# Nine matmuls on zeros ahead of the first real one, in place of fourteen

## The chip, the cores and the metric

The kernel runs on one core of one Trainium2 chip. The metric is the time of one execution on the device, in microseconds (us). The engines are TensorE (PE: matmuls; PEld: the loads of its stationary operand), VectorE (DVE), ScalarE (ACT), GpSimd (POOL) and the queue that issues most transfers (SP).

## The reference, cut to what matters

Attention through 32 landmarks (means over groups of 18 tokens), for 8 batches of 8 heads with 576 tokens of 64 channels, then a mixture of 8 experts in which each of the 4608 tokens goes to one expert:

```python
def _attn_ref(q, k, v):                       # each (8, 8, 576, 64)
    q_lm = q.reshape(B, H, m, S // m, D).mean(axis=3)
    k_lm = k.reshape(B, H, m, S // m, D).mean(axis=3)
    A = sm(q, k_lm)
    Bm = sm(q_lm, k_lm)
    C = sm(q_lm, k)
    Z = Bm.transpose(0, 1, 3, 2) / (norm1(Bm) * norminf(Bm) + 1e-06)
    for _ in range(6):
        Z = 2 * Z - Z @ Bm @ Z
    return A @ Z @ C @ v

def _moe_ref(x, w_gate, w1, w2):              # x (4608, 512); w1 (8, 512, 1024); w2 (8, 1024, 512)
    logits = x @ w_gate
    expert_idx = np.argmax(logits, axis=1)
    for e in range(E):
        mask = expert_idx == e
        h = np.maximum(x[mask] @ w1[e], 0.0)
        out[mask] = gate_w[mask, None] * (h @ w2[e])
    return out
```

(Here `norm1` and `norminf` stand for the two matrix norms, and `sm` for a softmax over scaled products.)

## The kernel before, in words

The kernel has two parts. In the first, attention, the work comes in quads: a quad is four heads of one batch, so there are 16 quads, and two quads make the pair of one batch. In the second, the experts, blocks of 128 tokens of one expert go through its two weight matrices.

Attention runs in periods. In period `i` the generator `front` turns keys and queries of quad `i` (line 123: three PE transposes of 96 columns for each head, by a product with the identity; line 124: ACT copies them out of PSUM, with two buffers of the tile `ps_tp`); `middle` makes the landmark means and the score products of quad `i-1` (lines 143, 171, 176) and their softmaxes; `values` multiplies quad `i-2` with its values (lines 255, 261, 269, 275); `back` iterates the inverse of a pair (line 319: eight products in turn, each followed by work of DVE and ACT on the tile `rp`) and applies it (line 359); `final` makes the rows of a pair (line 394: twelve matmuls; line 395: ACT copies them; line 400: SP stores them into `xs`). Keys, queries and values of a quad come in three transfers of 576 KB (line 112, tiles `ld_k`, `ld_q`, `ld_v`, two buffers each, so that the load for quad `i` waits until quad `i-2` has been read); the first two quads' come in halves of two heads. The values of the first quad are issued behind the queries of the third.

The order on each engine in this part isn't written out by hand. `merge` deals the steps of the generators of one period in proportion, each with a priority (a boost for `back` and `final`: `BOOST`), and the framework's scheduler (`schedule_with_timeline_sim=True`) then orders the instructions of every engine by its own estimate of when each can start. From the end of the periods on, the order of PE and SP, and later of the other engines, is the program's own (`manual_schedule`).

At the very beginning, while the first keys are on the way, PE multiplies a tile of zeros with itself. Nothing reads the products. They stand in the constructor of `Routing` (lines 480 to 484), and their number is a constant of the module, at line 35:

```python
        x = zero.bitcast(BF16)
        ps = self.p_ch.tile([128, 512], F32, name="ps_ch")
        for _ in range(WARM):
            nc.tensor.matmul(ps, lhsT=x[:, :128], rhs=x[:, :512], start=True, stop=True)
```

`ps` is a buffer of the pool `p_ch`, whose next user is the first product of line 319. `zero` is set by DVE (line 479) and is stored once (line 485) to clear a table.

Of the kernel before, what the change touches and what calls it, by code (L numbers as in the profile page):

```python
# [31 lines left out]
TAIL = 1  # L32
AHEAD = 0
WAIT = 0
WARM = 14
ROWS, FETCH = 15, 16


# [418 lines left out]
class Routing:  # L457


    def __init__(self, tc, ctx, front, psum, order):  # L460
# [21 lines left out]
# [3 lines that stand above are left out]
# [556 lines left out]
```

## Time and profile before

| | us |
|---|---|
| three runs | 695.89, 700.67, 702.92 (median 700.67) |
| the profiled execution | 696.69 |
| its span, first to last instruction | 694.9 |
| mean granted TensorE clock | 0.967 of 2.4 GHz |
| PE busy | 648.9 (93%) |
| DVE busy | 521.8 (75%) |
| ACT busy | 400.6 (58%) |
| POOL busy | 342.9 (49%) |

The execution is 1.8 us longer than its span: what lies ahead of the first and behind the last instruction. A busy share is that of instructions under way; the granted clock is a share of full speed, 2.4 GHz, and has two levels, 1.00 and 0.50 (1.2 GHz); a mean between them tells how much of a stretch lay at either.

### The profile page before, as it was taken

What the parts mean: (1) busy time and instruction counts of PE and PEld (TensorE: products, weight loads), DVE (VectorE), ACT (ScalarE), POOL (GpSimd) and SP (SyncE); (2) the same over time, 40 slices, a digit from 0 to 9 for tenths busy, and PEclk for the clock granted to TensorE, in tenths of its full rate; (3) what the DMA queues carried; (4) which work ended last, traced back from release to release, by engine and by line L of the source; (5) the groups of instructions that cost most, each with busy time, mean ns of one, the idle gap of its engine ahead of it and who ended that gap; (6) DMA issues with size and microseconds to landing.
All of it is one profiled execution on the core that took longest, in us unless ns stands there. A gap on an engine that the chain in (4) does not pass through costs nothing.

```text
span 694.9 us, 13825 instructions
## 1 busy us (share of the span) xinstructions
PE 648.9 (93%) x4489; PEld 510.0 (73%) x4489; DVE 521.8 (75%) x1409; ACT 400.6 (58%) x997; POOL 342.9 (49%) x371
## 2 busy tenths in 40 slices
PE   8899989999699868989999999999999999999996
PEld 4676757667476646867888888888888888888884
DVE  4788857769887977667699779857699699866653
ACT  4776656556655654345567576645467467544542
POOL 4554546357347263777546354453535445351231
PEclk9999989789889998999999999999999999999999
DMA  9996876668823550255143333411144243310010
GB/s 212 246 225 162 191 167 145 147 136 161 235 75 107 166 117 7 65 195 186 62 154 112 122 114 106 158 54 38 61 153 142 79 157 105 110 62 32 31 50 29
DMA packets 45482, 84.70 MB, mean 122 GB/s; under 512 B 8050, under 2 KB 26484, under 8 KB 45376
## 3 DMA queue, kind: packets, MB, share of 16 engines
q1 hardware_dynamic: 35328, 63.24, 34.4%
q0 software_dynamic: 10048, 20.29, 9.2%
q8 instruction: 38, 0.62, 0.4%
q14 instruction: 68, 0.56, 0.3%
HBM read 64.29 MB, written 19.73 MB: 121 GB/s over the span
## 4 chain that ended last, share of the span: by engine, by line
PE 46%; DMA 3%; issue 3%; POOL 1%; DVE 1%; ACT 0%; POOLq 0%; DVEq 0%
PE ps_fi L820 12%; PE ps_ch L820 12%; PE ps_fr L820 11%; PE ps_tp L820 11%; DMA xe<-xs,read 3%; DVE h L840 0%; POOL xg L788 0%; POOL out_dram L851 0%; POOL xe L788 0%; DVE buf L801 0%; DVE ht_lo L806 0%; ACT ht_hi L803 0%; POOLq L886 0%; POOLq L851 0%; DVEq L801 0%
## 5 line engine op out<-in xcount | busy, mean ns | idle before, releaser
L851 POOL DMA_INDIRECT out_dram<-buf,write x38 | 38.6, 1016 | 166.9 <-ACTq L777 141.0
L788 POOL DMA_INDIRECT xe<-xs,read x84 | 87.4, 1040 | 25.7 <-issue 23.8
L788 POOL DMA_INDIRECT xg<-xs,read x80 | 83.3, 1042 | 30.4 <-issue 23.0
L803 ACT CAST ht_hi<-buf 128x512 fp32r<-128x512 f32 x76 | 47.1, 622 | 71.5 <-DVE buf L801 70.5
L840 DVE TENSOR_SCALAR h<-ps_tp 32x256 f32<-32x256 f32 x152 | 64.2, 422 | 27.2 <-PE ps_tp L820 24.9
L840 DVE TENSOR_SCALAR h<-ps_fi 32x256 f32<-32x256 f32 x144 | 60.8, 422 | 28.5 <-PE ps_fi L820 26.1
L838 ACT ACTIVATE h<-ps_tp 32x256 f32<-32x256 f32 x152 | 57.1, 376 | 41.3 <-PE ps_tp L820 37.5
L838 ACT ACTIVATE h<-ps_fi 32x256 f32<-32x256 f32 x144 | 54.1, 376 | 34.5 <-PE ps_fi L820 30.7
L820 PE MATMUL ps_ch<-whi,ht_hi 128*128 128x512 f32 x152 | 59.8, 394 | 2.2 <-ACTq L777 2.2
L394 PE MATMUL ps_fi<-w,at 128*96 128x264 f32 x160 | 52.6, 424 | 9.4 <-DVE l L398 7.7
L820 PE MATMUL ps_fr<-whi,ht_hi 128*128 128x512 f32 x152 | 60.8, 400 | 0.0
L820 PE MATMUL ps_fr<-wlo,ht_hi 128*128 128x512 f32 x152 | 60.1, 395 | 0.0
L820 PE MATMUL ps_fr<-whi,ht_lo 128*128 128x512 f32 x152 | 59.8, 394 | 0.0
L820 PE MATMUL ps_ch<-wlo,ht_hi 128*128 128x512 f32 x152 | 59.5, 391 | 0.0
L820 PE MATMUL ps_ch<-whi,ht_lo 128*128 128x512 f32 x152 | 59.2, 389 | 0.0
L564 POOL DMA_INDIRECT order<-i_tok,l_at x48 | 44.8, 934 | 28.8 <-issue 10.9
L801 DVE STREAM_TRANSPOSE buf<-h 128x512 f32<-128x512 f32 x76 | 49.7, 690 | 5.7 <-DMA out_dram<-buf,write 1.9
L806 DVE TENSOR_TENSOR ht_lo<-buf,ht_hi 128x512 fp32r<-128x512 f32 x76 | 51.0, 692 | 3.7 <-ACT ht_hi L803 0.2
L765 DVE TENSOR_TENSOR wlo<-raw,whi 128x512 fp32r<-128x512 f32 (+1 forms) x64 | 48.8, 819 | 3.2 <-ACT whi L764 3.2
L820 PE MATMUL ps_tp<-whi,xt_hi 128*128 128x512 f32 x152 | 48.7, 401 | 2.2 <-ACTq L777 2.2
L820 PE MATMUL ps_tp<-whi,xt_lo 128*128 128x512 f32 x152 | 47.9, 396 | 0.0
L820 PE MATMUL ps_tp<-wlo,xt_hi 128*128 128x512 f32 x152 | 47.7, 396 | 0.0
(275 smaller groups left out, 1551.9 us busy)
## 6 DMA issues: line engine op xcount, KB each, us to landing
raw<-in_moe_w_dram SPq DMA_DIRECT2D x48, 512.0 KB, 9.4
xs<-xrow SPq DMA_DIRECT2D x44, 192.0 KB, 5.0
ld_k<-in_k_dram SPq DMA_DIRECT2D x14, 576.0 KB, 8.6
ld_q<-in_q_dram SPq DMA_DIRECT2D x14, 576.0 KB, 8.3
ld_v<-in_v_dram SPq DMA_DIRECT2D x14, 576.0 KB, 9.4
xe<-xs,read POOLq DMA_INDIRECT x84, 2.8
xg<-xs,read POOLq DMA_INDIRECT x80, 2.5
ld_k<-in_k_dram SPq DMA_DIRECT2D x4, 288.0 KB, 7.4
```

The costliest lines, as they stand in the source:

```text
L394: nc.tensor.matmul(po[g][:P96, :QUAD], lhsT=ats[g][:, n:n + 96], rhs=w[:, g, :], start=True, stop=True)
L564: self.nc.gpsimd.indirect_dma_start(out=self.places[n + j], out_offset=bass.IndirectOffsetOnAxis(ap=at[:, j:j + 1], axis=0), in_=self.tok[ ...
L765: (engine or nc.vector).tensor_tensor(out=l, in0=x, in1=h.bitcast(F32), op=ALU.subtract)
L788: self.nc.gpsimd.indirect_dma_start(out=x[:, t, :], out_offset=None, in_=src.rearrange("n (q c) -> (n q) c", q=4), in_offset=bass.Indirect ...
L801: nc.vector.transpose(out=x.rearrange("p c (t j) -> p t c j", t=4), in_=src[:, :, 32 * c:32 * c + 128].rearrange("p t (c i) -> p t c i", c=4))
L803: nc.scalar.copy(out=hi[:, c:c + 4, :], in_=x)
L806: nc.vector.tensor_tensor(out=lo[:, c:c + 4, :], in0=x, in1=hi[:, c:c + 4, :].bitcast(F32), op=ALU.subtract)
L820: nc.tensor.matmul(ps[c // 512] if type(ps) is list else ps[:, c // 512], lhsT=x0[:, a, :], rhs=w[:, a, c:c + 512], start=a == 0 and j == ...
L838: nc.scalar.activation(out=dst, in_=src, func=AF.Relu)
L840: nc.vector.tensor_scalar(out=dst, in0=src, scalar1=0.0, scalar2=None, op0=ALU.max)
L851: nc.gpsimd.indirect_dma_start(out=self.outs[s], out_offset=bass.IndirectOffsetOnAxis(ap=at, axis=0), in_=y, in_offset=None, bounds_check= ...
```

## The change

The number of products on zeros goes from fourteen to nine:

```diff
-WARM = 14
+WARM = 9
```

No other line differs. Since the order of attention is made by the scheduler from its estimates, the rest of the order moves too. First, what PE begins with (`zero`: the tile of zeros; `ld_k`, `ld_q`: keys and queries as loaded; `ls_k`: their sums for the landmarks). Before, the end of the fourteen and what follows:

```order
L484 MATMUL ps_ch<-zero 128x512
L123 MATMUL ps_tp<-ident,ld_k 128x96 x12
L123 MATMUL ps_tp<-ident,ld_q 128x96 x12
L123 MATMUL ps_tp<-ident,ld_k 128x96 x12
L143 MATMUL ps_fr<-ls_k,e_192 128x128
L123 MATMUL ps_tp<-ident,ld_q 128x96 x6
```

Now, the end of the nine and what follows:

```order
L484 MATMUL ps_ch<-zero 128x512
L123 MATMUL ps_tp<-ident,ld_k 128x96 x12
L123 MATMUL ps_tp<-ident,ld_q 128x96 x12
L123 MATMUL ps_tp<-ident,ld_k 128x96 x12
L123 MATMUL ps_tp<-ident,ld_q 128x96 x3
L143 MATMUL ps_fr<-ls_k,e_187 128x128
```

The transposes of the first two quads stand in the same order as before; only the first landmark product has moved behind three more of them.

Second, PE where the inverse of pair 0 is applied (line 359, reading `bdz`) and its first rows are made (line 394, reading `w` and `at`). Before, line 359 stands behind 141 transposes of line 123, of the 24 that each quad has, so late in the sixth quad, and line 394 begins behind 150:

```order
L123 MATMUL ps_tp<-ident,ld_q 128x96 x6
L269 MATMUL ps_fr<-ident,st 64x128
L359 MATMUL ps_ch<-st,bdz 128x72 x2
L123 MATMUL ps_tp<-ident,ld_q 128x96 x3
L123 MATMUL ps_tp<-ident,ld_k 128x96 x3
L275 MATMUL ps_fr<-wg,yt 32x8 x4
L171 MATMUL ps_sc<-T_q,lm_k 32x288 x8
L255 MATMUL ps_tp<-ident,ce 96x128 x3
L143 MATMUL ps_fr<-ls_k,e_192 128x128
L123 MATMUL ps_tp<-ident,ld_k 128x96 x3
L394 MATMUL ps_fi<-w,at 96x264
```

Now, line 359 stands behind 111 transposes, in the fifth quad, and line 394 begins behind 117:

```order
L171 MATMUL ps_sc<-T_k,lm_q 32x288 x8
L176 MATMUL ps_sc<-lm_k,lm_q 32x32 x4
L261 MATMUL ps_fr<-ld_v,ct 32x64 x5
L359 MATMUL ps_ch<-st,bdz 128x72 x2
L261 MATMUL ps_fr<-ld_v,ct 32x64 x19
L123 MATMUL ps_tp<-ident,ld_q 128x96 x6
L269 MATMUL ps_fr<-ident,st 64x128
L394 MATMUL ps_fi<-w,at 96x264 x2
```

The work of pair 0 has moved ahead by 30 transposes at line 359 and by 33 at the first matmul of line 394, a little over a quad. Its eight products of line 319 start behind 72 transposes, where they started behind 78, so that from the first of them to line 359 PE has 39 transposes, where it had 63. For later pairs the distance shrinks: the first rows of pair 1 come at 7.1 quads of transposes in place of 8.0, of pair 2 at 9.4 in place of 9.9, of pair 4 at 13.9 in place of 14.0.

Third, SP, the loads of quads 5 to 8 and the first stores of rows. Before:

```order
L112 DMA ld_q<-in_q_dram 96x4x384
L112 DMA ld_k<-in_k_dram 96x4x384
L112 DMA ld_v<-in_v_dram 96x4x384
L112 DMA ld_q<-in_q_dram 96x4x384
L400 DMA xs<-xrow 96x512
L112 DMA ld_k<-in_k_dram 96x4x384
L400 DMA xs<-xrow 96x512 x2
```

Now:

```order
L400 DMA xs<-xrow 96x512
L112 DMA ld_q<-in_q_dram 96x4x384
L400 DMA xs<-xrow 96x512
L112 DMA ld_k<-in_k_dram 96x4x384
L400 DMA xs<-xrow 96x512 x2
L112 DMA ld_v<-in_v_dram 96x4x384
L400 DMA xs<-xrow 96x512
L112 DMA ld_q<-in_q_dram 96x4x384
```

The first store now stands ahead of the queries of quad 6; before, it stood behind the queries of quad 7.

## Rows read from the trace of the kernel before

**Rows 1.** Busy time by stretch: us, busy of PE, PEld, DVE, ACT, POOL (count), PEclk, DMA share, GB/s.

```profile
0.00:8.00 8.00, 6.46 (x20) 2.67 (x20) 3.04 (x24) 1.36 (x2) 1.90 (x14) 1.00 0.80 195
8.00:48.00 40.00, 34.07 (x520) 25.45 (x518) 28.72 (x85) 28.86 (x90) 22.77 (x30) 1.00 1.09 239
48.00:128.00 80.00, 73.31 (x921) 55.26 (x920) 59.87 (x225) 50.39 (x165) 43.99 (x52) 0.94 0.72 166
128.00:148.00 20.00, 19.37 (x187) 15.12 (x187) 14.37 (x62) 10.25 (x30) 9.06 (x12) 0.66 0.52 120
148.00:233.00 85.00, 73.80 (x892) 54.71 (x885) 70.89 (x280) 52.19 (x165) 44.99 (x50) 0.92 0.57 141
313.00:695.00 382.00, 374.81 (x1632) 306.25 (x1632) 286.35 (x523) 220.62 (x457) 172.82 (x165) 1.00 0.29 96
```

**Rows 2.** Timeline of PE, 0 to 82 us: start, us, instruction [idle before, releaser].

```profile
1.54 6.10 PE L484 MATMUL ps_ch<-zero 128*128 128x512 bf16 x14 [1.54 <-DVE zero L479]
7.47 0.66 PE L123 MATMUL ps_tp<-ident,ld_k 96*128 96x96 f32 x6
...
9.33 0.77 PE L123 MATMUL ps_tp<-ident,ld_q 96*128 96x96 f32 x6 [0.19 <-ACT T_k L124]
...
12.20 0.77 PE L123 MATMUL ps_tp<-ident,ld_k 96*128 96x96 f32 x6 [0.19 <-ACT T_k L124]
...
14.11 0.77 PE L123 MATMUL ps_tp<-ident,ld_q 96*128 96x96 f32 x6
...
20.98 0.41 PE L261 MATMUL ps_fr<-ld_v,ct 96*32 96x64 f32 x10 [0.61 <-DMA ld_v<-in_v_dram]
...
28.62 0.54 PE L319 MATMUL ps_ch<-bt 128*128 128x160 f32 x2 [0.18 <-POOL bt L295]
...
54.92 0.86 PE L359 MATMUL ps_ch<-st,bdz 128*128 128x72 f32 x4 [1.58 <-DVE bdz L347]
...
64.59 1.05 PE L394 MATMUL ps_fi<-w,at 128*96 128x264 f32 x4
...
67.24 0.72 PE L123 MATMUL ps_tp<-ident,ld_q 96*128 96x96 f32 x6
```

**Rows 3.** Timeline of PEld, the spacing of the last products on zeros.

```profile
6.21 0.15 PEld L484 LDWEIGHTS <-zero 128*128 128x128 bf16 x1 [0.28 <-issue]
6.64 0.15 PEld L484 LDWEIGHTS <-zero 128*128 128x128 bf16 x1 [0.28 <-issue]
```

**Rows 4.** Chain that ended last, a piece in the experts' part.

```profile
341.32 5.51 PE ps_fi L820 x24
```

**Rows 5.** Timeline of SP, loads of quad 1 and of quad 6's queries.

```profile
2.68 0.94 SPq L112 DMA_DIRECT2D ld_k<-in_k_dram  x2
3.67 1.01 SPq L112 DMA_DIRECT2D ld_q<-in_q_dram  x2
...
45.70 0.31 SPq L112 DMA_DIRECT2D ld_q<-in_q_dram  x1
```

**Rows 6.** DMA issues, quad 1: KB each, median us to landing.

```profile
ld_k<-in_k_dram SPq DMA_DIRECT2D x2, 288.0 KB, 7.4
ld_q<-in_q_dram SPq DMA_DIRECT2D x2, 288.0 KB, 8.1
```

**Rows 7.** Line 319, 0 to 240 us: PE idle before it, us and times, until.

```profile
  DVE rp L337: 5.5, 8
```

**Rows 8.** Busy time by microsecond where the clock fell and rose; columns as in rows 1.

```profile
55.00:56.00 1.00, 1.00 (x7) 1.00 (x8) 1.00 (x5) 0.95 (x4) 0.31 (x1) 0.62 1.02 255
58.00:59.00 1.00, 1.00 (x7) 0.98 (x8) 1.00 (x3) 0.31 (x2) 0.00 (x0) 0.67 0.89 312
130.00:131.00 1.00, 1.00 (x11) 0.76 (x11) 0.96 (x7) 0.79 (x4) 0.00 (x0) 0.67 0.06 16
143.00:144.00 1.00, 1.00 (x5) 0.62 (x3) 0.00 (x0) 0.27 (x1) 0.88 (x1) 0.51 0.00 0
```

**Rows 9.** Timeline of PE inside the low stretch, transposes of line 123.

```profile
137.20 0.69 PE L123 MATMUL ps_tp<-ident,ld_k 96*128 96x96 f32 x3
```

## Prediction

> **What bounds the kernel now.** I read the busy time by stretch first [rows 1], since one share for the whole span hides stages with different limits. The last 382 us, the experts' matmuls, have PE busy for 374.81 us at a granted clock of 1.00. They follow attention as a whole: if attention ends earlier or later, this part moves with it and keeps its length. So all that the change can do is done in the first 233 us or so, where the scheduler orders the instructions.
>
> That part has three limits in turn. Up to 48 us the DMA share stands at 1.09 (0.80 in the first 8 us, when the first transfers start) with 239 GB/s: the transfers have no free time, while PE is busy for 34.07 of 40 us. From 48 to 233 us the DMA share falls to 0.72 and less, and PE is busy for 73.31 + 19.37 + 73.80 = 166.5 of 185 us, so 18.5 us idle. And the clock is at 1.00 only in part: means of 0.94, 0.66 and 0.92 over 80, 20 and 85 us, with one level at 0.50, make 9.6 + 13.6 + 13.6 = 36.8 us at the lower level. If PE alone set the pace there, half of that, 18.4 us, would be lost. These two sums, idle time and low clock, are what another order can win or lose.
>
> Then the timeline of PE at the start [rows 2]: the fourteen products go from 1.54 us to 7.64, and the first transposes follow without a gap. Nothing else waits for the products, and their number sets when the transposes begin.
>
> **The products themselves.** Their spacing is 0.43 us for 512 columns [rows 3]. In the experts' part 24 matmuls of 512 columns take 5.51 us, 0.23 us each, at a granted clock of 1.00 [rows 1, 4]. So all of the fourteen ran at the lower of the two levels, though the clock column gives 1.00 for the first 8 us: it shows no fall where none was recorded. The first transposes ran at full speed, 0.66 us for six [rows 2], against 0.69 us for three where the clock was low [rows 9]. So the clock rose at the very end of the fourteen. Removing five takes 5 x 0.43 = 2.1 us, and the transposes can begin at about 5.3 us, if the first keys are there; their transfer is issued 2 us ahead of quad 1's keys, which land at 10.6 (below), and its data were in use at 7.47.
>
> **What is late next.** The transfers do not start earlier: the first is issued at the start whatever PE does, and their path is full [rows 1]. The second half of quad 1's keys is issued at about 3.2 us and lands 7.4 us later, at 10.6; that of its queries at about 4.2, landing 8.1 later, at 12.3 [rows 5, 6] (the issue times are those of the second transfer of each pair). Their transposes start now at 12.20 and 14.11 [rows 2]. So there is 1.6 to 1.8 us of room, and of the 2.1 us at most about 1.6 passes this point. At 20.98 us PE waits 0.61 us for the values of quad 0 [rows 2]. Those are seventh in line behind the keys and queries of three quads on a path that is full from the start, so they land at the same time in the changed kernel, and PE would wait the 1.6 us more there. My value for the early start is therefore 0; the bounds are -2.1 us (all of it goes through, because other work fills the wait) and 0.
>
> **The moved order.** The change also redeals attention. The two places that I can put a price on are in the order shown above: the first rows of pair 0 (line 394) come behind 117 transposes in place of 150, and SP has a store ahead of the queries of quad 6. The twelve matmuls of a pair cost 12 x 1.05 / 4 = 3.2 us of PE [rows 2]. They and their copies move toward the stretch before 48 us, where the transfers set the pace and PE has 5.9 us idle [rows 1]; what is done there needn't be done later. But DVE is busy for 28.72 of the same 40 us and ACT for 28.86, and the rows of a pair need both, so I take half: -1.5 us, with 0 and -3.2 as bounds. The store ahead of quad 6's queries can delay their load, but that load is issued at 45.70 us and first used at 67.24 [rows 2, 5], with some 8 us to landing [rows 6], so some 13 us of delay are covered and I take 0 for it. All other moved rows can't be priced one by one. Their bound is what one bad stretch costs: the clock fell at 130.3 us and rose at 144.0 [rows 8], 13.6 us at the lower level with PE busy almost throughout [rows 1], or 6.8 us lost. One such stretch more or fewer is my bound for the rest of the order, +6.8 to -6.8; value taken 0, as nothing in the order says which.
>
> Is nine enough for the clock? The row says that the fourteen raised it only at their end, and the nine end 2.1 us before that. What follows them is dense, but it is transposes, and in the stretch from 130 to 144 us the clock stayed at 0.50 for 13 us with PE busy and with many transposes in it [rows 8, 9]. The Trainium skill's page "TensorE: Matmul & The Clock Gate" (Part 4: PE-mode transpose) says that transposes don't count as activity that lifts the clock in the way matmuls do. By that rule the change would leave the first two quads at the lower level; the trace agrees in so far as the long low stretch was full of transposes, though other matmuls stood there too. From 55.2 to 58.7 us a mix of transposes and matmuls did raise it [rows 8]. I take it that the clock rises after nine, soon behind them, at no cost, and keep the other case as a rival.
>
> **The sum.** 0 for the start, -1.5 us for pair 0, 0 for the rest: -1.5 us. On the profiled execution that is 696.69 - 1.5 = 695.2 us. That execution is 4 us under the median of the three runs, 700.67. The four known times are 695.89, 696.69, 700.67 and 702.92, with 698.7 in the middle, and I make the forecast there: 698.7 - 1.5 = 697.2, so 697 us.
>
> **The rivals.** First, the new order also loses a bad stretch. For it: there are 18.5 us of idle time and 36.8 us of low clock to be had, and pair 0 being ahead gives PE other work to do at waits. Against: the later pairs are hardly ahead (by 0.1 of a quad at pair 4), so past 100 us the order has the same kind of waits. It gives 697.2 - 6.8 = 690.4 us.
>
> Second, slower: pair 0's inverse becomes a chain of exposed waits. Place: the eight products of line 319 and line 359 of pair 0, each of which needs DVE's answer to the one before. Between the first and line 359 PE had 63 transposes' worth of other work; now it has 39. Eight times in attention PE idled before line 319 for DVE's `rp`, 5.5 us in all, 0.69 each [rows 7], and at line 359 of pair 0 it waited 1.58 us, after which the clock fell at 55.2 us until 58.7 [rows 2, 8]. Nine waits of 0.69 are 6.2 us, and one such fall costs half of 3.4 us, 1.7. Without the gain of 1.5 us that is 698.7 + 7.9 = 706.6 us. It decides as soon as DVE's answer takes longer than the PE work that now stands between two steps. That is about 1.8 us: from 28.6 to 54.9 us [rows 2] it took 26.3 us for 63 transposes' worth, so 39 are 16.3 us, over nine steps. Against it: the waits come in a stretch that the transfers limit anyway, so a part is paid from idle time.
>
> Third, the clock stays low behind the nine. Then the 16 heads of quads 0 and 1, which go at 0.47 us a head now (four heads from 7.47 to 9.33 us [rows 2]), take at most 0.69 each [rows 9]: +3.5 us, or nothing if ACT's copies still set the pace. Less the 2.1 us of the earlier start, that is at most +1.4, and a few matmuls behind them up to 21 us may add 0.6. With pair 0's -1.5: up to 698.7 + 2.0 - 1.5 = 699.2 us.
>
> Fourth, the change does nothing: the start is lost at the values' wait and pair 0's advance is worth nothing, 698.7 us. I count this with the forecast.
>
> **How the numbers follow.** The forecast, with the fourth rival, gets 0.44; the better order 0.27; the exposed chain or an equal bad stretch elsewhere 0.21; the low clock 0.08. A measurement of this kernel can tell about 1% from no change, some 7 us: its own runs lie 7 us apart. The better order at -6.8 - 1.5 us is beyond that bound, and a part of the forecast's own spread too: faster 0.29. The exposed chain is slower by a little over 1%: 0.21. The rest, 0.50, is within 1%. The range reaches to both of these cases with a little for their spread: 689 to 707 us. The forecast's own range is 694 to 701 us.
>
> **What would show it.** In the changed kernel's profile: the first transposes at 5.3 us, and six of them in 0.66 to 0.77 us if the clock has risen, over 0.9 if not. A wait for the values of quad 0 that ends near 21 us and lasts some 2 us. DMA share still near 1.09 up to 48 us. Line 359 of pair 0 near 45 us in place of 54.9. The time under low clock in the first 233 us against 36.8 us, and PE's idle time from 48 us on against 18.5, say which of the orders came out. The experts' part should keep its length. The forecast is wrong if the start of the experts' dense stretch moves by more than 7 us either way, or if the early gain of 2 us is still there at 48 us.

## The result, and the profile after

The changed kernel takes 706.9 us (median of 21 runs, 699.98 to 710.93), the kernel before, run beside it, 703.6 us (21 runs, 692.92 to 709.35). The ratio is 1.0102, with a 95% interval of 1.0077 to 1.0128: slower by some 7 us. (The ratio is of the runs within 1.5% of each kernel's fastest alone, 10 of the 21 of before and 20 of the 21 of the changed kernel; over all runs the means are 702.5 and 706.0 us, so 3.6 us apart, slower as well.) I had forecast 697 us and a gain of 1.5 us. The time is at the upper edge of the range, the sign is wrong.

The profiled execution of the changed kernel has a span of 705.8 us, 10.9 more than before. This is more than the two kernels differ by: the profiled execution of before (696.69 us) lies 6.9 us under the median of its 21 runs, that of the changed kernel (707.58) 0.7 above its own. What follows is about these two executions. First the busy time by stretch, with the columns of [rows 1]:

```profile
0.00:8.00 8.00, 6.42 (x25) 3.18 (x25) 3.05 (x24) 2.88 (x6) 1.90 (x15) 1.00 0.80 193
8.00:48.00 40.00, 34.21 (x369) 24.94 (x369) 23.36 (x64) 21.23 (x65) 16.87 (x22) 0.70 0.88 194
48.00:128.00 80.00, 75.67 (x957) 55.74 (x956) 62.94 (x233) 52.11 (x170) 44.77 (x54) 0.96 0.73 169
128.00:148.00 20.00, 18.25 (x221) 15.16 (x223) 15.86 (x56) 12.69 (x42) 13.24 (x16) 0.83 0.68 163
148.00:233.00 85.00, 77.77 (x909) 56.09 (x894) 69.53 (x279) 52.56 (x162) 44.55 (x51) 0.88 0.57 146
233.00:313.00 80.00, 69.20 (x359) 51.73 (x359) 57.30 (x220) 34.43 (x89) 40.37 (x41) 0.87 0.27 81
313.00:695.00 382.00, 377.55 (x1646) 308.68 (x1645) 293.90 (x537) 225.36 (x467) 180.44 (x174) 1.00 0.31 102
```

The second row is where it shows. PE is as busy as before from 8 to 48 us (34.21 against 34.07 us) and does 369 matmuls in place of 520; its clock is at 0.70 on average and was at 1.00. The path of the transfers, which had no free time there (1.09, 239 GB/s), is at 0.88 with 194 GB/s. From 128 to 148 us the changed kernel is better off (0.83 against 0.66). From 233 to 313 us, a stretch that I had not looked at, its clock is at 0.87; before it was at 0.96:

```profile
233.00:313.00 80.00, 67.08 (x331) 50.51 (x329) 58.60 (x214) 36.96 (x92) 47.32 (x50) 0.96 0.37 115
```

The dense stretch of the experts can be told by the first long run of 24 matmuls in the chain of waits (start, us, what). It begins at 313.24 us before and at 324.47 after, 11.2 us later:

```profile
313.24 5.73 PE ps_ch L820 x24
```

```profile
324.47 5.75 PE ps_ch L820 x24
```

What follows has the same length: 694.9 - 313.24 = 381.7 us before, 705.8 - 324.47 = 381.3 after. So the whole loss lies ahead of it, and the move is beyond the 7 us that I had set as a sign of being wrong. Up to there PE did the same work (2857 and 2852 matmuls recorded, the five products apart). The busy time of both, of before and then of after:

```profile
0.00:313.24 313.24, 274.09 (x2857) 203.71 (x2857) 235.73 (x887) 180.16 (x541) 170.28 (x207) 0.93 0.63 154
```

```profile
0.00:324.47 324.47, 289.57 (x2852) 212.81 (x2853) 239.94 (x887) 181.43 (x541) 170.56 (x207) 0.88 0.59 148
```

PE is busy 15.5 us longer and idle 4.3 us less (34.90 against 39.15), which makes the 11.2. It did not wait more; the same matmuls took longer, at the lower of the two clock levels. By microsecond windows, half of PE's busy time at that level is 20.6 us before and 36.5 after, 15.9 more. Taken together with the idle time, the stretch to 48 us costs 10.6 us, 48 to 233 us gives back 5.9, and the rest up to the dense stretch costs 6.9.

The timeline of PE at the start answers to [rows 2]:

```profile
1.54 4.02 PE L484 MATMUL ps_ch<-zero 128*128 128x512 bf16 x9 [1.54 <-DVE zero L479]
5.35 2.12 PE L123 MATMUL ps_tp<-ident,ld_k 96*128 96x96 f32 x12
7.49 1.90 PE L123 MATMUL ps_tp<-ident,ld_q 96*128 96x96 f32 x12
9.40 2.40 PE L123 MATMUL ps_tp<-ident,ld_k 96*128 96x96 f32 x12
...
12.12 0.68 PE L143 MATMUL ps_fr<-ls_k,e 128*128 128x128 f32 x2
...
30.73 1.17 PE L123 MATMUL ps_tp<-ident,ld_q 96*128 96x96 f32 x6
...
52.38 0.67 PE L359 MATMUL ps_ch<-st,bdz 128*128 128x72 f32 x4
```

The transposes begin at 5.35 us, 2.1 us earlier, as forecast, and the second twelve go at 0.475 us a head, the pace of before. The first twelve are slower, at 0.53 us a head: the clock came up among them. The third twelve take 2.40 us. In the microsecond windows the clock falls at 9.98 us and rises at 23.6:

```profile
9.00:10.00 1.00, 0.98 (x7) 0.61 (x8) 0.95 (x3) 0.84 (x3) 0.94 (x1) 0.99 1.09 243
10.00:11.00 1.00, 1.00 (x6) 0.72 (x6) 0.31 (x1) 0.69 (x2) 0.84 (x3) 0.50 1.06 235
...
23.00:24.00 1.00, 1.00 (x16) 0.69 (x15) 0.97 (x2) 0.47 (x1) 0.00 (x0) 0.69 1.09 240
```

So there were two suspects at once: the clock, which falls behind nine products, and the order, which the scheduler deals anew for nine. The experiments take them apart.

### The profile page after: what moved, and what is told of

It is laid out like the page before. It is cut to its first block, busy times and chain, and to the rows that moved or that the text cites. A ratio compares the mean times of both kernels' runs of the same rounds, so it can differ in the third digit from the quotient of the medians.

```text
span 705.8 us, 13822 instructions
## 1 busy us (share of the span) xinstructions
PE 664.0 (94%) x4484; PEld 519.3 (74%) x4484; DVE 526.0 (75%) x1409; ACT 402.0 (57%) x997; POOL 343.5 (49%) x371
## 4 chain that ended last, share of the span: by engine, by line
PE 45%; DMA 4%; issue 3%; DVE 1%; POOL 1%; ACT 0%; POOLq 0%; DVEq 0%
PE ps_fi L820 12%; PE ps_ch L820 12%; PE ps_tp L820 11%; PE ps_fr L820 11%; DMA xg<-xs,read 4%; DVE h L840 0%; POOL out_dram L851 0%; POOL xg L788 0%; DVE buf L801 0%; DVE ht_lo L806 0%; ACT ht_hi L803 0%; POOLq L886 0%; POOLq L851 0%; DVEq L801 0%; DVEq L777 0%
## 5 line engine op out<-in xcount | busy, mean ns | idle before, releaser
L838 ACT ACTIVATE h<-ps_fi 32x256 f32<-32x256 f32 x144 | 54.1, 376 | 34.8 <-PE ps_fi L820 31.1
```

Of the source, the lines that this page charges most:

```text
L838: nc.scalar.activation(out=dst, in_=src, func=AF.Relu)
```

## The experiments

They ran on several chips. On some of them every kernel takes some 5% longer (the kernel before 739 to 742 us); so each is compared by its ratio to the kernel before on the same chip, from 4 to 14 runs of each variant. e13 to e15 ran on a chip like that of the result, the others on chips with the longer times; the one profile of the kernel before is from the former kind.

### The number and the order apart

A function that runs behind the scheduler adds products on zeros, or takes some out, and leaves the order of everything else on every engine as it is (`ADD` is -5, +5 or, in e4, +10; the label of e4 is misleading, its order is that of nine):

```diff
+def products(nc, add):
...
+    names = {i.ins.name for i in WARMING}
...
+        pair = [(pe[pe.index(k) - 1], k) for k in mine]
+        if add < 0:
+            gone = {k for p in pair[add:] for k in p}
+            insts = [i for k, i in enumerate(insts) if k not in gone]
+        else:
+            more = [copy.replace(insts[k], name=nc.get_next_instruction_name()) for _ in range(add) for k in pair[-1]]
+            insts[mine[-1] + 1:mine[-1] + 1] = more
+        block.instructions = insts
```

> The order of every engine as with fourteen products, five of the products taken out behind the scheduler: only the number changes. Theory A (the order made the loss): the time stays within 0.4% of before, ratio 0.996 to 1.004. Theory B (nine products don't hold the clock up over the first transposes): the ratio is 1.007 to 1.013, as with the change itself, and the profile shows the granted clock at 0.50 for 10 us or more between 8 and 25 us. Both: between the two. In all, the first transposes begin at 5.3 us.

Measured: 1.0027 (0.9988 to 1.0065).

> The order of every engine as with nine products, five products added behind the scheduler. Theory A (order): the ratio stays at 1.008 to 1.015, with PE's wait of some 3 us for ACT's softmax near 27 to 30 us still there. Theory B (clock): the ratio falls to 0.996 to 1.004, and the clock stays at 1.00 over the first 25 us. In both the first transposes begin at 7.5 us.

Measured: 1.0142 (1.0088 to 1.0197). The wait was not there as expected: it is 1.02 us, and the loss is as large.

> The changed kernel as it is, beside the other two on the same chip: ratio 1.008 to 1.013 by all theories. By theory B its profile shows a low clock between 8 and 25 us again; by theory A that was chance and may be gone with the time unchanged.

Measured: 1.0163 (1.0123 to 1.0204), above the range that I had set for all theories.

> The order as with nine products, with nineteen products (ten added behind the scheduler): the transposes begin 4.3 us later than in the changed kernel. If what the products hold up passes through to the end, the time is 2 us above that of the kernel with fourteen in this order; if the loads' path hides it, within 1 us of it. Theory A: ratio 1.008 to 1.018. Theory B: 0.998 to 1.006.

Measured: 1.0118 (1.0050 to 1.0185).

The order of nine is slower with nine, fourteen and nineteen products; the order of fourteen is not measurably slower with nine (0.65% at most, by the interval). So the loss is the order's, and the number is worth nothing that these runs can tell. The busy time by stretch of e1 shows that nine products raise the clock and that it stays up in the other order:

```profile
8.00:48.00 40.00, 33.60 (x519) 25.37 (x520) 30.37 (x91) 28.61 (x90) 22.47 (x31) 1.00 1.09 245
```

And its timeline of PE shows the early start and where most of it is lost, at the loads (e6 below, with fourteen products and two more in the same order, begins its transposes at 7.21 us and has neither wait; it issues the keys of quad 5 at 29.18 us, e1 at 29.05):

```profile
5.12 0.66 PE L123 MATMUL ps_tp<-ident,ld_k 96*128 96x96 f32 x6
...
14.42 0.44 PE L123 MATMUL ps_tp<-ident,ld_k 96*128 96x96 f32 x3 [0.99 <-DMA ld_k<-in_k_dram]
...
19.25 0.41 PE L261 MATMUL ps_fr<-ld_v,ct 96*32 96x64 f32 x10 [0.79 <-DMA ld_v<-in_v_dram]
```

### Is it the early fall of the clock?

In the order of nine the first landmark product (line 143) stands behind three more transposes, and in the four profiles with that order the clock had fallen by then; in the two with the order of fourteen it held. That made theory C: the fall in this stretch of transposes is the price. e5 to e7 put two products between the transposes; e8 starts PE cold.

```diff
+AT = [12, 24]
...
+        for n in sorted(AT, reverse=True):
...
+            both = [copy.replace(i, name=nc.get_next_instruction_name()) for i in pattern]
...
+            insts[at + 1:at + 1] = both
```

> The changed kernel, its order untouched, with two products on zeros more, one behind the 12th transpose of PE's row and one behind the 24th; nothing reads them. Theory C (the order of nine costs time because PE has nothing but transposes for 6 to 7 us behind the first products, the clock falls there, and that stretch is lost): the clock stays at 1.00 past 12 us, and the ratio to the kernel before falls from 1.016 to between 0.995 and 1.004. Rival D (the other waits of that order are the price, and the fall of the clock lies beside them): the clock may stay up, and the ratio stays at 1.010 to 1.016.

Measured: 1.0175 (1.0120 to 1.0230). The clock stays up to 17.5 us, as meant, and falls then; nothing is won.

> The kernel before, its order and its fourteen products untouched, with the same two products more. Theory C with a chance in it (some executions of the kernel before lose the clock early too, which is why its times lie far apart): 0.995 to 1.000, and times closer together. Rival (the kernel before never loses the clock in its first transposes): 1.000 to 1.002, two products being 0.4 us of PE.

Measured: 1.0010 (0.9970 to 1.0051), which doesn't tell the two apart.

> The kernel before in its order, with nine products at the start and the same two between the transposes. Theory C: the clock stays up, as behind fourteen; 0.993 to 1.000. If nine products leave the clock less sure than fourteen even with the two: 1.003 or more and a fall of the clock before 12 us in the profile.

Measured: 1.0026 (0.9982 to 1.0071). Neither of the two cases: in its profile the clock falls at 15.2 us, behind the two products, for 17 us.

> The kernel before in its order with one product at the start in place of fourteen, so that PE comes to the transposes at the low clock. Theory C (a low clock over the first stretch is the price, whatever the order): the clock is at 0.50 from the start to beyond 10 us, and the ratio is 1.010 to 1.016. Rival D (the waits of the order of nine are the price): the clock is as low, but the ratio stays under 1.005, since this order has none of those waits.

Measured: 1.0090 (1.0051 to 1.0129). This is neither of the two values that I had set: a cold start has a price of its own in the good order, about two thirds of that of the new order. PE waits for the identity and then makes twelve transposes in 2.43 us, where six took 0.66 before [rows 2]; it keeps this pace to about 16 us:

```profile
1.54 0.61 PE L484 MATMUL ps_ch<-zero 128*128 128x512 bf16 x1 [1.54 <-DVE zero L479]
4.29 2.43 PE L123 MATMUL ps_tp<-ident,ld_k 96*128 96x96 f32 x12 [2.15 <-POOL ii L473]
```

### Other orders

The scheduler gives another order for nearly every number of products, and they come in two families (a row is a run of like instructions). For 8, 10 and 14 to 18 products line 359 of pair 0 stands at row 89 to 91 of PE, for 0 to 7, 9 and 11 to 13 at row 68 to 70; nineteen lies between, at 74. Four runs take orders from both. The edit is the constant and, for e9 and e10, products added behind the scheduler so that there are fourteen:

```diff
-WARM = 14
+WARM = 13
...
+ADD = 1
```

> The order that the scheduler gives for thirteen products, with fourteen products at the start. PE's row is that of the kernel before up to the first value products of line 261 (the first landmark product behind 36 transposes, quad 2's keys behind lines 171 and 176); behind that it is nearly that of the changed kernel, with pair 0's inverse and line 359 ahead (row 68 of PE, in place of row 89). Theory F (the price is that pair 0's chain stands ahead of other work and sets the pace, whatever happens in the first 15 us): 1.010 to 1.016. Theories C and D (the price is the stretch of pure transposes, or the wait for quad 2's keys, both before 18 us): 0.997 to 1.004.

Measured: 1.0104 (1.0067 to 1.0141).

> The order that the scheduler gives for six products, with fourteen at the start: the first landmark product behind only 33 transposes, earlier than in the kernel before, and pair 0 ahead as in the changed kernel (line 359 at row 68). Theory F: 1.010 to 1.016. Theory C: 0.995 to 1.002, since the stretch of pure transposes is the shortest.

Measured: 1.0286 (1.0243 to 1.0328). This is outside both ranges, nearly twice the upper end of F's loss.

> Eight products in place of fourteen, and the order that the scheduler gives for them: that of the kernel before but for three transposes of keys and three of queries in the first 50 rows of PE; line 359 of pair 0 comes behind as much work as before. Theory F: 0.996 to 1.004, the number of products and the early rows being worth nothing. Rival (fewer products than fourteen cost time by themselves): 1.006 or more.

Measured: 1.0003 (0.9966 to 1.0040).

> Ten products, and the order for them: that of the kernel before up to row 407 of PE (pair 5), a different one behind it. Theory F: 0.996 to 1.006, with what the rows behind pair 5 are worth as its spread. Rival (any number but the tuned fourteen loses): 1.010 or more.

Measured: 1.0025 (0.9993 to 1.0058).

So theories C and D can't be the whole price: e9 has neither the fall nor the wait before 18 us, and loses. The busy time from 8 to 48 us, of e9 and then of e11:

```profile
8.00:48.00 40.00, 33.10 (x442) 24.84 (x440) 25.61 (x74) 24.96 (x78) 18.97 (x24) 0.91 0.87 207
```

```profile
8.00:48.00 40.00, 35.65 (x494) 26.47 (x493) 26.16 (x79) 26.25 (x84) 21.21 (x28) 0.83 1.02 234
```

e11 has the lower clock of the two (0.83) and is as fast as before; e9 keeps the clock at 0.91 and loses a per cent. (e11 does 494 matmuls at 0.83 and e9 442 at 0.91, so the count of matmuls is not the clock's alone either.) What goes with the time in these two rows is not the clock but the transfers' share, 0.87 against 1.02.

### One place on DVE, and pair 0

In e9, at full clock, PE waits 3.00 us where it waited 0.98 before:

```profile
27.25 0.72 PE L171 MATMUL ps_sc<-T_q,lm_k 64*32 64x288 f32 x16 [3.00 <-ACT be L197]
```

The timeline of the changed kernel says why on DVE: quad 0's sums (line 231) stand ahead of quad 1's maxima (line 186) and wait for ACT, and the maxima, whose scores are there, wait behind them; the last line is PE's wait there:

```profile
23.34 0.75 DVE L226 TENSOR_REDUCE a_mx<-a 128x18 f32<-128x576 f32 x1
26.08 0.75 DVE L231 TENSOR_REDUCE a_sm<-a 128x18 f32<-128x576 f32 x1 [1.99 <-ACT a L228]
...
27.26 0.69 DVE L186 TENSOR_REDUCE c_mx<-ps_sc 128x1 f32<-128x576 f32 x1
...
29.86 0.72 PE L171 MATMUL ps_sc<-T_q,lm_k 64*32 64x288 f32 x16 [3.01 <-ACT be L197]
```

In the kernel before the maxima come first, at 23.35 us, and PE's wait is short (timelines of DVE and of PE):

```profile
23.35 0.76 DVE L186 TENSOR_REDUCE c_mx<-ps_sc 128x1 f32<-128x576 f32 x1 [1.93 <-PE ps_sc L176]
...
25.06 0.74 DVE L231 TENSOR_REDUCE a_sm<-a 128x18 f32<-128x576 f32 x1
...
26.34 0.72 PE L171 MATMUL ps_sc<-T_q,lm_k 64*32 64x288 f32 x16 [0.98 <-ACT be L197]
```

e13 turns that place round with one edge of issue order, e15 forces it into the kernel before, and e14 is an order without it that has pair 0 ahead all the same (`WARM = 19`, `ADD = -5`). The edge of e13:

```diff
+        r = v.tensor_scalar(out=mx[:, a:e], in0=mx[:, a:e], scalar1=-0.125, scalar2=None, op0=ALU.mult)
+        if i == 1:
+            self.tc.add_manual_dep(self.held, r.ins.name, mybir.DependencyInfo(
+                mybir.DependencyClass.NoSync, mybir.DependencyReason.DATA))
...
+        r = nc.vector.tensor_reduce(out=sm, in_=a, axis=AX.X, op=ALU.add)
+        if i == 0:
+            self.held = r.ins
```

and of e15 (where `held` is quad 0's line 233):

```diff
+            with self.tc.issue_after(self.held) if i == 1 else nullcontext():
+                v.tensor_reduce(out=mx[:, 0:1], in_=outer, axis=AX.XY, op=ALU.max)
```

> The changed kernel with one edge of order more: on DVE quad 0's line 231 is issued behind quad 1's line 189. The rows of PE are those of the changed kernel but for one product of line 319, those of ACT and SP are the same, on POOL line 234 stands three rows later. Theory G (the loss is that one place on DVE and what waits behind it): PE's wait of 3.0 us before line 171 shrinks to some 1 us, and the ratio falls from 1.016 to 1.000 to 1.006. Theory F (the rest of the order, with pair 0 ahead, is the price): the wait shrinks likewise, and the ratio stays at 1.009 to 1.016.

Measured: 1.0130 (1.0065 to 1.0195). The wait is gone and the loss is not; the timeline of PE in e13 (line 200 is line 197 of before):

```profile
26.06 1.23 PE L171 MATMUL ps_sc<-T_q,lm_k 64*32 64x288 f32 x16 [0.63 <-ACT be L200]
```

> The order that the scheduler gives for nineteen products, with fourteen at the start: on DVE quad 1's maxima stand ahead of quad 0's sums as in the kernel before, but pair 0's line 359 comes at row 74 of PE, nearly as early as in the changed kernel, and the pairs behind it at other rows than in either. Theory G: 0.997 to 1.005. Theory F: 1.008 to 1.016.

Measured: 1.0254 (1.0183 to 1.0326), above F's range.

> The kernel before with fourteen products, and quad 1's line 186 issued on DVE behind quad 0's line 233, as in the changed kernel; the scheduler deals all rows behind it anew (line 359 of pair 0 at row 74). Theory G and theory F both: slower, 1.006 to 1.016; a ratio under 1.004 would say that neither this place nor pair 0 ahead has a price by itself.

Measured: 1.0216 (1.0152 to 1.0280), above the range; as the edge deals all later rows anew, this run doesn't price the place by itself.

The place on DVE is not the price: the loss stays without it (e13) and comes without it (e14). Theory F was left, pair 0 ahead. e16 and e17 hold pair 0's chain alone behind as many transposes as in the kernel before, by edges on PE:

```diff
+BEHIND = ((14, 12), (16, 15), (17, 16), (18, 16), (20, 16), (20, 18), (21, 20), (24, 21), (24, 23))
...
+        for n, (k, q) in enumerate(BEHIND):
+            for name, m in (("k", k), ("q", q)):
+                for r in self.links[2 * n:2 * n + 2]:
+                    self.tc.add_manual_dep(r, self.turned[(m - 1) // 4, name, (m - 1) % 4].name, order)
```

> The changed kernel with edges of order on PE alone: each product of pair 0's chain (line 319, nine of them with the last two counted as one step, and line 359) is issued behind as many transposes of line 123 as in the kernel before; the scheduler deals the rest. Line 359 of pair 0 stands at row 86 in place of 68; the place on DVE (sums ahead of maxima) stays as in the changed kernel. Theory F (pair 0 ahead is the price): 0.997 to 1.005. Rival H (pair 0 only goes along with a worse deal of the rest, and any deal but the one of before loses): 1.009 to 1.020.

Measured: 1.0200 (1.0157 to 1.0242).

> Six products, and the same edges in the order that the scheduler gives for six (that order alone was at 1.0286). Line 359 of pair 0 at row 86. Theory F: 0.997 to 1.007. Rival H: 1.015 to 1.030.

Measured: 1.0213 (1.0179 to 1.0247).

> The changed kernel as it is, on the same chip as the two. It was at 1.010 and 1.016; 1.008 to 1.018 expected by all theories.

Measured: 1.0159 (1.0127 to 1.0191).

Theory F falls too: with pair 0 held back the order of nine is no better. (The edges hold it further back than meant: line 359 comes at 59.74 us in e16 and 57.97 in e17, where e1 has it at 53.19, and the rest is dealt anew. So a price of pair 0 ahead, exchanged for one of pair 0 late, isn't excluded.) Rival H is left, with a limit: the orders of eight and ten, which differ from that of before in a few rows or far behind, lose nothing. No single place that was tried is the price.

### What the slower orders share

In all profiles side by side, one thing goes with the ratio better than the clock up to 48 us does: when SP issues the keys of quad 5 (line 112), and whether the path of the transfers then has a hole. SP's timeline, first of before, then of the changed kernel; the keys of quads 4, 5 and 6:

```profile
22.56 0.32 SPq L112 DMA_DIRECT2D ld_k<-in_k_dram  x1
...
30.78 0.31 SPq L112 DMA_DIRECT2D ld_k<-in_k_dram  x1
...
40.02 0.31 SPq L112 DMA_DIRECT2D ld_k<-in_k_dram  x1
```

```profile
25.61 0.32 SPq L112 DMA_DIRECT2D ld_k<-in_k_dram  x1
...
41.06 0.31 SPq L112 DMA_DIRECT2D ld_k<-in_k_dram  x1
...
50.60 0.31 SPq L112 DMA_DIRECT2D ld_k<-in_k_dram  x1
```

That load needs the buffer of quad 3's keys, so it waits for their last transposes. Before, PE makes the last of these in this row, which begins 0.46 us ahead of the load:

```profile
30.32 0.42 PE L123 MATMUL ps_tp<-ident,ld_k 96*128 96x96 f32 x3
```

In the changed kernel it has pair 0's chain between them, and the low clock besides, and the last row ends the wait:

```profile
33.91 0.74 PE L123 MATMUL ps_tp<-ident,ld_k 96*128 96x96 f32 x3
...
36.44 1.22 PE L319 MATMUL ps_ch<-rp 128*128 128x128 f32 x4
37.45 0.69 PE L123 MATMUL ps_tp<-ident,ld_k 96*128 96x96 f32 x3
...
39.00 1.27 PE L319 MATMUL ps_ch<-rp 128*128 128x160 f32 x4
40.06 0.97 PE L123 MATMUL ps_tp<-ident,ld_k 96*128 96x96 f32 x6
```

The longest of SP's waits for PE (total, times, longest) is 8.7 us (before, 5.0), and meanwhile the transfers nearly stand still, a share of 0.25 from 33 to 42 us, where it was 1.09 before:

```profile
SPq L112 <- PE ps_tp L123: 28.5, 8, 8.7
```

```profile
33.00:42.00 9.00, 8.62 (x74) 7.07 (x73) 5.73 (x20) 4.04 (x11) 2.82 (x4) 0.57 0.25 66
```

| order, products | keys of quad 5 issued, us | share of transfers, 8 to 48 us | clock, 8 to 48 us | ratio |
|---|---|---|---|---|
| e1, of 14, nine | 29.1 | 1.09 | 1.00 | 1.0027 |
| e11, of 8, eight | 33.0 | 1.02 | 0.83 | 1.0003 |
| e9, of 13, fourteen | 36.7 | 0.87 | 0.91 | 1.0104 |
| e16, of 9, pair 0 held | 37.4 | 0.88 | 0.70 | 1.0200 |
| e13, of 9, DVE place turned | 39.0 | 0.88 | 0.79 | 1.0130 |
| e3, of 9, nine | 39.8 | 0.89 | 0.66 | 1.0163 |
| e15, of 14, DVE place forced | 33.9 | 0.89 | 0.91 | 1.0216 |
| e14, of 19, fourteen | 31.1 | 0.97 | 0.96 | 1.0254 |

Orders with a share of 1.02 or more are between 1.0003 and 1.0027, but for the cold start of e8 (1.07, and 1.0090). Those below are at 1.0102 or more. Among these the share doesn't order the losses: e4 has the lowest (0.84) and 1.0118, e10 has 0.91 and the largest, 1.0286. e14 says too that this is not all: it has most of its transfers in time and is among the slowest. Nor does pair 0's chain alone hold the load: with the chain held back (e16) the keys of quad 5 are still issued at 37.4 us. No run changed the hole alone, by a third buffer for keys for instance, so it stands as what the traces show together, and not as a cause that was tried. Nor does it say how large a loss will be.

Over a whole execution the clock does go with the time. With one and the same order, the kernel before beside e13 to e15 took 691.71 us at a mean clock of 0.975 and 702.04 at 0.960. Beside e18 its runs have 0.932 on average, the changed kernel's 0.915. That isn't all of the loss either: e17, beside the same runs, has 0.925 and is no faster than e18 (1.0213 against 1.0159). Whether an order costs time by the clock that it gets after 48 us was not tried.

None of the eighteen beat the kernel before.

## Why the prediction was wrong, step by step

- **The products and the early start.** Right. Transposes at 5.35 us (forecast 5.3). With the order kept (e1) most of the early start is lost at the loads, as the section on what is late next had it: 0.99 us at the keys of quad 2, which it did not name, and 0.79 at the values of quad 0, where it had put some 2 us. The time is that of before. The value 0 for the early start holds.
- **"The clock rises after nine, soon behind them, at no cost."** It rises (e1, and the changed kernel within its first transposes). In the new order it fell again at 9.98 us, which is the third rival's case by another road. I had priced that rival at 2.0 us at most, and the runs differ on it: e11 spends a third of the 40 us from 8 to 48 us at the lower level and loses no time, while e8, cold from the start to about 16 us, loses some 7 us. Why the two differ is open. The rule of the Trainium skill's page "TensorE: Matmul & The Clock Gate" (Part 4: PE-mode transpose) that I weighed would leave the first quads at the lower level. The traces agree in part: in e1 the clock stays at 1.00 through 5.2 us of nothing but transposes (5.29 to 10.50 us), up to the first landmark product; in the changed kernel, where that product comes at 12.12 us, it falls behind 4.4 us of them (5.56 to 9.98 us).
- **Pair 0's advance, -1.5 us.** Wrong. Line 359 came at 52.38 us, 2.5 us earlier, not 10, and nothing was won by 48 us. I had said that PE's 5.9 idle us there would take pair 0's work. In the profile it stands between the transposes of quad 3's keys, and what I left out is that a transpose moved back can hold a load back, on a path that I had just called full (0.88 in place of 1.09). But the advance is not shown to be the price: with pair 0 held back (e16, e17) the loss stays.
- **"All other moved rows can't be priced one by one... value taken 0."** This is the step that failed. With the number of products worth nothing that can be measured (e1), the moved order is worth +1.0 to +1.6%, 7 to 12 us (3.6 over all runs of the first measurement), where I took 0 and a bound of 6.8. It is not in the first rows of PE alone, since e9 has those of before and loses 1.0%, while e11 has others and loses nothing. Which of the moved rows cost it stays open. I read the order of PE and SP only; the flip on DVE that comes first was not looked at, though e13 says that it isn't the price. And I set 0 between a gain and a loss, where no order tried here gains: seven others that the scheduler or an edge gave lie between 1.010 and 1.029, those of eight and ten at 1.000 and 1.003.
- **The second rival** (slower, 706.6 us) has the right time by luck, with the wrong place: I put the loss into waits before line 319, and PE waits less than before (34.90 us up to the dense stretch, against 39.15).
- **The limits of the argument.** "All that the change can do is done in the first 233 us" is wrong: in the profiled pair another 6.9 us went from 233 us to the dense stretch. From 48 to 233 us, where I had looked for what could be won, the changed kernel in fact gained 5.9. The experts' part kept its length, as said.
- **The base.** 698.7 us was 4.9 under the 703.6 us of 21 runs. So of the 9.7 us from the sum's 697.2 to 706.9, half is the base, 1.5 the gain that did not come, and 3.3 the difference of the two medians.

## What to carry to other kernels

A change that only alters an estimate of the scheduler's is a change of the whole order: separate the two, by adding or removing the instructions behind the scheduler, before any mechanism is believed. Where a stretch is bound by transfers into a few buffers, look for the load that waits for a moved row before counting on the engine's idle time (the traces here suggest it; no run tried it alone). And a long stretch at the low clock, however striking in the profile, is not by itself the price of a change: look for a kernel that has it and isn't slower.

## What was not expected of the hardware

The granted clock fell in the midst of dense work: in the changed kernel PE is busy for 0.98 us of the microsecond ahead of the fall. In e1 it stayed at 1.00 through 5.2 us of transposes alone (5.29 to 10.50 us). In the order of nine it fell at 9.6 to 13.0 us in all five profiles of that order as it is (the changed kernel, e2, e3, e4, e18), and with two products between the transposes at 17.5 us (e5).

A program that keeps PE cold at its start (e8) loses 0.9% (0.5 to 1.3), some 7 us. Going from fourteen products to eight loses nothing that can be measured (e11, e1).

In the clock column PE reads 1.00 from the start until the first fall, even in e8, where twelve transposes took 2.43 us: the level at the beginning is to be read from durations.
